# Block-sparse attention and a gated MLP on one core: from split fp32r attention to plain float32 in tiles of the TensorE array

## Chip, cores and metric

One core of one Trainium2 chip runs the whole program. The metric is the time of one execution on the device in microseconds (us), measured as a median over several runs. The profile is one execution recorded by the hardware profiler.

## What is computed

The reference, cut to what matters (4 batches, 8 heads, 768 positions, head size 64; d_model 512, d_ff 1024):

```python
def _attn_ref(q, k, v, n_global, n_local):          # 8 and 96
    scores = scale * np.matmul(q, k.transpose(0, 1, 3, 2))
    is_global = pos[None, :] < int(n_global)
    is_local = (rel >= 0) & (rel < int(n_local))
    keep = is_global | is_local
    scores = np.where(keep, scores + bias, -1e9)    # bias: a slope per head times the distance
    a = softmax(scores)
    return np.matmul(a, v)

def _moe_ref(x, w_in, w_spatial, b_spatial, w_out):
    h = np.maximum(x @ w_in, 0.0)
    u, v = h[..., :d_ff // 2], h[..., d_ff // 2:]
    v_n = (v - mean) / np.sqrt(var + 1e-06)
    v_s = np.einsum('ts,bsd->btd', w_spatial, v_n) + b_spatial[None, :, None]
    return (u * v_s) @ w_out
```

## The kernel before

**Blocks.** Attention goes over 24 blocks of 128 queries, n = 6 b + i (batch b, block i of the batch). A block sees its own 128 keys and the 128 before them, in whose first 32 places the global keys stand, so 256 keys; the first block of a batch sees 128. Heads go in four pairs g: a pair fills the 128 partitions, 64 for each head.

**A block's steps.** prep (L681) loads q and k and prep_v (L718) loads v. scores (L742) multiplies q by k for each head into a PSUM tile of tag "s"; VectorE adds the bias and takes the row's extreme (pr<-s, mn), ScalarE takes the exponential and sums it up (pr<-pr,mn), and GpSimd multiplies by the reciprocal of the sum (pr<-pr,rc), except in batch 0, where that factor is applied to the output ("folded", L664). values (L808) transposes the probabilities on TensorE (p<-ident,pr), copies them to SBUF (pth<-p) and multiplies them by v into ops. The outcome, transposed, is split into an fp32r upper and lower part (xth, xtl), with which the MLP works.

**Two ways through attention.** For batch 0 (whole(n), L660) the products are in plain float32. There q stands in a tile with 64 rows of zeros for the other head, so that a score product uses all 128 rows, and the product with v computes both heads' columns for both heads' probabilities (128 x 256) and uses half. A plain float32 product is two LDWEIGHTS and two MATMUL instructions. For batches 1 to 3, q, k, v and the probabilities are split into two fp32r parts. Six splitting instructions and twelve DMAs per block put q's and k's parts under one another so that the 64 rows of both parts fill 128 rows; a score takes two matmuls, a product with v takes two for each head, and three adds on VectorE and ScalarE (c<-ops) join the parts. TensorE's instructions per full block: 16 for scores and 16 with v, in both ways, and 16 transposes.

**MLP.** mlp_v (V), mlp_u (U), mlp_s (G) and mlp_o (O), L889 to L968, use fp32r in three passes (upper x upper, upper x lower, lower x upper) into PSUM tiles of tag "m". w_in arrives as 64-bit floats and is converted and split by split_weights (L615); so is w_out, and w_spatial is split. This setup (tokens I, Q, T, B) lies in batch 0.

**Order.** Nothing is issued while the kernel is written down: Recorder keeps every operation (L58), plan (L287) simulates the five engines with the costs of cost (L195) and ranks each token by KEYS (L432), and the outcome is one fixed order for every engine. keep_warm (L396) puts transposes of the identity (s<-ident and m<-ident, results that nobody reads) into gaps of TensorE. All instructions are issued at L39, so the profile shows L39 everywhere, and its groups are told apart by tile names. Tensor engine results go to eight PSUM banks: two for each of s, p, ops and m.

## Time and profile before

| | us |
|---|---|
| median of 3 runs | 475.75 |
| lowest and highest run | 473.37, 476.11 |
| span of the profiled execution | 473.8 |
| TensorE busy (matmul) in it | 460.7 |
| VectorE busy | 344.6 |
| ScalarE busy | 279.9 |
| GpSimd busy | 254.1 |

The page lists the span of the profiled execution, from its first to its last instruction, and no other time for it; the span lies within the times of the three runs. PE is the matmul side of TensorE, PEld its weight loads, DVE VectorE, ACT ScalarE, POOL GpSimd, SP the engine that issues DMAs. The end of a matmul in the trace is modelled, so busy shares and means of PE include the tail of one matmul beside the start of the next; the spacing of starts tells what one costs in a run.

### The profile page before, as it was taken

The numbers are of one execution on the slowest core, as the hardware profiler recorded it, in microseconds if no ns is written. First come the engines' busy times: TensorE is split into PE (matmuls) and PEld (weight loads), VectorE is DVE, ScalarE is ACT, GpSimd is POOL, SyncE is SP. The second block draws the span as 40 slices with busy tenths as digits, with TensorE's granted clock in tenths as the row PEclk, the third lists the DMA queues.
The fourth block names the chain that finished last, engine by engine and source line by source line (L and its number), as shares of the span: only waits on it lengthen the run. The fifth ranks groups of instructions, "written<-read, shape, count | busy, mean of one in ns | idle before, by whom it ended". The sixth has DMA issues, their size and how long they took to land.

```text
span 473.8 us, 9730 instructions
## 1 busy us (share of the span) xinstructions
PE 460.7 (97%) x3181; PEld 424.3 (90%) x3181; DVE 344.6 (73%) x1016; ACT 279.9 (59%) x775; POOL 254.1 (54%) x378
## 2 busy tenths in 40 slices
PE   7889999999999999999999999999999999999995
PEld 6668888999999889999999999999989899999994
DVE  6899998948679987986766668784376998843332
ACT  5859896455477776786446448872155888721111
POOL 4334743377575788788545357883037775650000
PEclk9999999999999999999999999999999999999999
DMA  6947323747758687746582167630077683000111
GB/s 212 318 155 229 116 65 114 193 108 183 184 148 226 166 226 193 172 129 166 150 219 101 49 184 187 177 98 19 22 183 209 176 213 78 13 1 1 46 46 50
DMA packets 35915, 65.48 MB, mean 138 GB/s; under 512 B 6064, under 2 KB 6320, under 8 KB 35856
## 3 DMA queue, kind: packets, MB, share of 16 engines
q1 hardware_dynamic: 35856, 64.77, 49.7%
q8 instruction: 27, 0.44, 0.4%
q14 instruction: 32, 0.26, 0.2%
HBM read 29.76 MB, written 6.68 MB: 77 GB/s over the span
## 4 chain that ended last, share of the span: by engine, by line
PE 87%; DVE 4%; SPq 3%; DMA 2%; ACT 2%; issue 1%; DVEq 0%
PE m L39 61%; PE ops L39 9%; PE s L39 9%; PE p L39 8%; SPq L39 3%; DMA vring<-in_v_dram 2%; DVE c L39 1%; ACT pr L39 1%; DVE raw L39 1%; DVE ev L39 0%; DMA kring<-rawh 0%; DVE pr L39 0%; DVE w_in_h L39 0%; DVE rawh L39 0%; DVE xtl L39 0%
## 5 line engine op out<-in xcount | busy, mean ns | idle before, releaser
L39 ACT ACTIVATE pr<-pr,mn 128x256 f32<-128x256 f32 (+1 forms) x192 | 92.0, 483 | 17.5 <-DVE mn L39 17.1
L39 DVE TENSOR_TENSOR c<-ops,c 64x256 f32<-64x256 f32 x168 | 70.6, 421 | 11.0 <-ACT c L39 4.7
L39 DVE CUSTOM_DVE_ANT_0 pr<-s,bias 128x256 f32<-128x256 f32 (+1 forms) x192 | 68.6, 394 | 11.0 <-PE s L39 8.4
L39 POOL TENSOR_SCALAR pr<-pr,rc 128x256 f32<-128x256 f32 (+1 forms) x144 | 68.1, 493 | 10.4 <-DVE rc L39 8.3
L39 PE MATMUL s<-kring,q 128*128 128x256 f32 (+1 forms) x384 | 69.8, 307 | 1.3 <-DVE mn L39 1.0
L39 PE MATMUL ops<-pth,vring 128*128 128x256 f32 x352 | 67.0, 311 | 0.7 <-DVE pth L39 0.5
L39 PEld LDWEIGHTS s<-kring,q 128*128 128x128 f32 x384 | 57.6, 191 | 7.1 <-DVE mn L39 2.4
L39 ACT ACTIVATE pth<-p 128x512 fp32r<-128x512 f32 (+3 forms) x96 | 52.3, 559 | 15.1 <-PE p L39 11.5
L39 PEld LDWEIGHTS ops<-pth,vring 128*128 128x128 f32 x352 | 53.1, 189 | 5.4 <-DVE pth L39 1.2
L39 PE MATMUL p<-ident,pr 128*128 128x128 f32 x352 | 56.6, 273 | 0.7 <-ACT c L39 0.7
L39 DVE TENSOR_TENSOR pth<-p,pth 128x512 fp32r<-128x512 f32 (+1 forms) x72 | 45.1, 642 | 7.0 <-ACT pth L39 6.0
L39 DVE TENSOR_TENSOR ev<-m,b_bc 128x512 f32<-128x512 f32 x24 | 16.6, 691 | 46.1 <-PE m L39 46.0
L39 PEld LDWEIGHTS p<-ident,pr 128*128 128x128 f32 x352 | 42.2, 140 | 5.2 <-ACT c L39 1.3
L39 ACT ACTIVATE ev<-m 128x512 f32<-128x512 f32 (+1 forms) x36 | 21.3, 591 | 42.8 <-PE m L39 40.8
L39 PE MATMUL m<-w_t_h,vnh 128*128 128x256 f32 x288 | 43.9, 282 | 0.0
L39 PE MATMUL m<-w_t_h,vnl 128*128 128x256 f32 x288 | 43.7, 282 | 0.0
L39 PE MATMUL m<-w_t_l,vnh 128*128 128x256 f32 x288 | 43.7, 283 | 0.0
L39 POOL TENSOR_TENSOR xtl<-c,xth 128x256 fp32r<-128x256 f32 x40 | 29.8, 747 | 25.2 <-ACT xth L39 25.1
L39 ACT ACTIVATE gh<-ev 128x512 fp32r<-128x512 f32 x24 | 15.1, 630 | 42.6 <-DVE ev L39 42.6
L39 PEld LDWEIGHTS m<-w_t_h,vnh 128*128 128x128 f32 x288 | 38.9, 189 | 0.7
L39 ACT ACTIVATE c<-ops 64x256 f32<-64x256 f32 x72 | 27.3, 380 | 20.4 <-PE ops L39 17.9
L39 POOL TENSOR_TENSOR vnl<-ev,vnh 128x512 fp32r<-128x512 f32 x24 | 31.1, 1296 | 14.7 <-ACT vnh L39 9.4
(138 smaller groups left out, 997.8 us busy)
## 6 DMA issues: line engine op xcount, KB each, us to landing
q<-rawh SPq DMA_DIRECT2D x72, 128.0 KB, 2.4
q<-raw SPq DMA_DIRECT2D x72, 128.0 KB, 2.4
out_dram<-ev SPq DMA_DIRECT2D x23, 256.0 KB, 2.8
raw<-in_q_dram SPq DMA_DIRECT2D x18, 256.0 KB, 2.9
raw<-in_v_dram SPq DMA_DIRECT2D x18, 256.0 KB, 3.0
raw<-in_k_dram SPq DMA_DIRECT2D x18, 256.0 KB, 3.3
kring<-rawh SPq DMA_DIRECT2D x36, 128.0 KB, 2.4
kring<-raw SPq DMA_DIRECT2D x36, 128.0 KB, 2.4
```

Of the source, the lines that this page charges most:

```text
L39: getattr(self.real, self.call)(*self.args, **self.kw)
```

## The change

All 24 blocks go one way, in plain float32, with no split of q, k, v or the probabilities. q and k are loaded as they lie in memory, one DMA each; v too. The scores of a pair are two float32 products, each of 64 rows (its head's) of the array: tiles in rows. The products with v are of 64 columns each (its head's): tiles in columns. The score products of a whole block (8; in blocks 0 and 1 of half a block) are recorded as one operation `together`, and so are the 16 products with v, after all four transposed tiles are copied. The PSUM banks are now four for s, two for p (in which ops stands too) and two for m. Folding of the reciprocal stays with batch 0 (FOLD). The copy of pth, the normalisation and the upper part of x may go to either of several engines ("x" in CFG). The planner knows of `together`, of a time to change the array's shape, and of new KEYS; so the order of everything is new.

```diff
-CFG = {... 'pth': 'a', ... 'norm': 'p', ... 'xbh': 'a', ... 'b_pth': 2, 'b_c1': 3, ...}
+CFG = {... 'pth': 'x', ... 'norm': 'x', ... 'xbh': 'x', ... 'b_pth': 5, 'b_c1': 2}
...
-BUFS = {"gh": 1, "gl": 1, "u": 3, "s": 2, "p": 2, "m": 2, "raw0": 1, "raw1": 1, "rawh0": 1, "rawh1": 1}
+BUFS = {"gh": 1, "gl": 1, "u": 3, "s": 4, "p": 2, "m": 2, "wos": 2, "wc": 4}
...
+FOLD, SMALL = range(6), 2
+KEYS = {...}
...
     def issue(self):
-        getattr(self.real, self.call)(*self.args, **self.kw)
+        for call, args, kw in self.calls():
+            getattr(self.real, call)(*args, **kw)
...
+        if op.call == "together":
+            return sum(max(2 * elements(kw["rhs"]) * .422, 54) for _, _, kw in op.args), 0, False
...
+def shape_of(op):
+    if op.eng != "tensor":
+        return 0, 0
+    if op.call != "together":
+        return 0, 149 if op.call == "transpose" else 197
+    w = op.args[0][2]["lhsT"]
+    return (1, 197) if list(w.ap)[0][1] < P else (2, 143)
...
+        if e == "tensor" and op.mode != mode:
+            op.busy += op.load
+            mode = op.mode
...
     def prep(n):
...
+        nc.sync.dma_start(out=ring["q", n % 2], in_=q[b, i])
+        nc.sync.dma_start(out=ring["k"][:, n % 3], in_=k[b, i])
+        return ring["q", n % 2]
...
     def prep_v(n):
...
+        nc.sync.dma_start(out=ring["v"][:, n % 3], in_=v[b, i * P:(i + 1) * P, :])
...
     def scores(n, qt):
...
+        PAIRS = 2 if n < SMALL else 4
         for g in range(NP):
             if g == 2:
                 yield
-            sp = ps_s.tile([P, 2, W], F32, name="sp", tag="s")
-            for j in range(2):
-                h = 2 * g + j
-                if whole(n):
-                    nc.tensor.matmul(sp[:, j], lhsT=q1[:, j, g], rhs=kring[:, sl, g], start=True, stop=True)
-                    continue
-                for y, a in enumerate((q1, ql)):
-                    nc.tensor.matmul(sp[:, j], lhsT=a[:, j, g], rhs=kring[:, sl, j, g], start=(y == 0), stop=(y == 1))
+            if g % PAIRS == 0:
+                sp = [ps_s.tile([P, 2, W], F32, name="sp", tag="s") for _ in range(PAIRS)]
+                nc.together(nc.tensor, [
+                    ("matmul", (sp[x // 2 * 2 + j][:, x % 2],), dict(lhsT=qt[s_, g + x], rhs=kring[s_, sl, g + x], start=True, stop=True))
+                    for x in range(PAIRS) for j, s_ in enumerate(halves)
+                ])
...
     def values(n):
...
+            t = work.tile([P, nch, 2, P], F32, name="pth", bufs=nb("pth"))
+            cp(E("pth", g), t, pt)
+            pth.append(t)
...
+        ops = ps_p.tile([P, NP, P], F32, name="ops", tag="p")
+        nc.together(nc.tensor, [
+            ("matmul", (ops[s_, g],), dict(
+                lhsT=vring[:, order[c], g * P + 64 * j:g * P + 64 * j + 64], rhs=pth[g][:, c, j],
+                start=(c == 0), stop=(c == nch - 1),
+            ))
+            for g in range(NP) for c in range(nch) for j, s_ in enumerate(halves)
+        ])
+        if folded(n):
+            xs = work.tile([P, NP, P], F32, name="xs", tag="c1", bufs=nb("c1"))
+            nc.vector.tensor_tensor(out=xs, in0=ops, in1=div, op=ALU.mult)
+            hi_lo(xs, xh[:, :, toks], xl[:, :, toks], E("xf0h"), E("xf0l"))
+        else:
+            hi_lo(ops, xh[:, :, toks], xl[:, :, toks], E("xbh"), nc.vector)
-            pth = work.tile([P, 2 * nch, 2, P], F32R, name="pth", bufs=nb("pth"))
-            hi_lo(pt.rearrange("p c j x -> p (c j) x"), pth[:, :, 0], pth[:, :, 1], E("pth", g), nc.vector)
...
-                for j, s_ in enumerate(halves):
-                    cp(E("c1", j), c1[s_], opsring[j][halves[1 - j], :, 0:P])
-                for j, s_ in enumerate(halves):
-                    nc.vector.tensor_tensor(out=c1[s_], in0=opsring[j][s_, :, P:], in1=c1[s_], op=ALU.add)
-                for j, s_ in enumerate(halves):
-                    nc.vector.tensor_tensor(out=c1[s_], in0=opsring[j][s_, :, 0:P], in1=c1[s_], op=ALU.add)
-                hi_lo(c1, xh[:, gs, toks], xl[:, gs, toks], E("xbh", g // 2), E("xbl", g // 2))
```

## Rows read from the trace of the kernel before

**Rows 1.** The page, part 1: busy us (share of the span) xinstructions.

```profile
PE 460.7 (97%) x3181; PEld 424.3 (90%) x3181; DVE 344.6 (73%) x1016; ACT 279.9 (59%) x775; POOL 254.1 (54%) x378
```

**Rows 2.** Stretches of 25 us from the start: busy time by engine; the answer names the columns.

```profile
core 0: us, PE busy (x) PEld busy (x) DVE busy (x) ACT busy (x) POOL busy (x), PEclk, DMA share, GB/s
0.00:25.00 25.00, 20.54 (x108) 17.11 (x108) 19.15 (x91) 17.38 (x61) 9.03 (x21) 1.00 0.84 266
25.00:50.00 25.00, 22.56 (x125) 18.41 (x123) 24.39 (x68) 18.96 (x56) 12.29 (x12) 1.00 0.55 182
50.00:75.00 25.00, 25.00 (x151) 21.88 (x150) 23.34 (x76) 20.68 (x56) 13.93 (x17) 1.00 0.29 93
75.00:100.00 25.00, 25.00 (x163) 22.93 (x163) 20.23 (x50) 11.61 (x25) 11.78 (x17) 1.00 0.54 144
```

**Rows 3.** TensorE's waits from 50 us on: waiter <- waited for: us, times, longest.

```profile
PE ops L39 <- DVE pth L39: 0.5, 1, 0.5
PE s L39 <- DMA kring<-rawh: 0.2, 1, 0.2
```

**Rows 4.** The chain that ended last, pieces: start us, us, what.

```profile
8.12 9.48 DMA vring<-in_v_dram
...
82.63 1.73 PE ops L39 x8
...
125.98 0.87 PE p L39 x8
...
131.25 0.95 PE s L39 x8
```

**Rows 5.** Timeline, single matmul and weight loads: start us, us, what, [idle before].

```profile
44.80 0.38 PE L39 MATMUL s<-kring,q 128*128 128x256 f32 x1
...
61.43 0.30 PEld L39 LDWEIGHTS ops<-pth,vring 128*128 128x128 f32 x2 [0.28 <-ACT pth L39]
...
17.14 0.20 PEld L39 LDWEIGHTS p<-ident,pr 128*128 128x128 f32 x2 [0.47 <-ACT c L39]
```

**Rows 6.** TensorE's groups by form: xcount | busy us, mean ns of one | idle before.

```profile
L39 PE MATMUL ops<-pth,vring 128*128 128x256 f32 x352 | 67.0, 311 | 0.7 <-DVE pth L39 0.5 <-ACT pth L39 0.2
...
L39 PEld LDWEIGHTS s<-kring,q 128*128 128x128 f32 x384 | 57.6, 191 | 7.1 <-DVE mn L39 2.4 <-POOL xtl L39 0.6 <-issue 0.3
...
L39 PEld LDWEIGHTS p<-ident,pr 128*128 128x128 f32 x352 | 42.2, 140 | 5.2 <-ACT c L39 1.3 <-ACT pth L39 0.4
```

**Rows 7.** Stretches: first the instructions of ops alone, then all, after batch 0's attention.

```profile
0.00:50.00 50.00, 11.01 (x42) 7.34 (x42) 5.03 (x12) 0.00 (x0) 1.00 0.70 224
50.00:84.00 34.00, 11.22 (x46) 8.25 (x46) 4.18 (x10) 0.00 (x0) 1.00 0.31 97
...
84.00:474.00 390.00, 383.65 (x2750) 358.76 (x2748) 270.16 (x766) 217.61 (x593) 216.63 (x326) 1.00 0.49 131
```

**Rows 8.** VectorE's and ScalarE's groups by form, columns as in rows 6.

```profile
L39 DVE TENSOR_TENSOR c<-ops,c 64x256 f32<-64x256 f32 x168 | 70.6, 421 | 11.0 <-ACT c L39 4.7 <-ACT pth L39 1.3 <-PE ops L39 1.0
L39 DVE CUSTOM_DVE_ANT_0 pr<-s,bias 128x256 f32<-128x256 f32 x160 | 60.8, 416 | 6.1 <-PE s L39 4.8 <-POOL xtl L39 0.5 <-PE p L39 0.3
L39 DVE TENSOR_TENSOR pth<-p,pth 128x512 fp32r<-128x512 f32 x60 | 40.2, 687 | 5.0 <-ACT pth L39 4.2
...
L39 DVE TENSOR_TENSOR ev<-m,b_bc 128x512 f32<-128x512 f32 x24 | 16.6, 691 | 46.1 <-PE m L39 46.0
...
L39 DVE DVE_READ_ACCUMULATOR2_ANT mn<- 128x1 f32 x192 | 15.7, 82 | 0.0
...
L39 DVE TENSOR_TENSOR raw<-raw,rawh 128x512 fp32r<-128x512 f32 x15 | 13.1, 876 | 0.1
...
L39 ACT ACTIVATE pth<-p 128x512 fp32r<-128x512 f32 x60 | 34.5, 594 | 8.6 <-PE p L39 6.6 <-PE ops L39 1.1
```

**Rows 9.** The page, part 6: DMA issues by tile, xcount, KB each, us to landing.

```profile
q<-rawh SPq DMA_DIRECT2D x72, 128.0 KB, 2.4
...
kring<-rawh SPq DMA_DIRECT2D x36, 128.0 KB, 2.4
```

## Prediction

> **What bounds the kernel now.** I read the page first: PE is busy 460.7 of 473.8 us, and no other engine over 73% [rows 1]. Busy PE is not yet PE at its limit, so I went to the stretches and then to TensorE's waits. [...] Ahead of 50 us it is otherwise: there TensorE is busy 43.1 of 50 us, and VectorE 24.39 of 25 from 25 to 50 us [rows 2].

> [...] The chain gives the spacing of matmuls, as a run of n divided by n [rows 4]: a plain float32 pass (batch 0; every float32 product is two of them) over 256 columns 1.73/8 = 0.216 us; a split fp32r matmul over 256 columns 0.95/8 = 0.119; a transpose 0.87/8 = 0.109. One matmul's record is 0.38 us long at a spacing of 0.216 [rows 5]: the remaining 0.16 us is a tail that overlaps with the next. Two loads of 128 columns of weights with nothing before them lie 0.30 - 0.19 = 0.11 us apart; for the transposes, 0.20 - 0.14 = 0.06 [rows 5, 6]. In a run these loads hide: the spacing stays at 0.216.

> **What the change removes from TensorE.** Attention's products are 384 instructions of scores and 352 with v [rows 6]. Batch 0 (float32, 96 and 88 of them): scores 80 x 0.216 = 17.3 and 16 narrow ones (128 columns) at half, 1.7; v 88 x 0.216 = 19.0; together 38.0 us. Batches 1 to 3: scores 240 x 0.119 = 28.6 and 48 narrow ones, which cannot go below their 0.11 us load, 5.3; v 264 x 0.119 = 31.4; together 65.3. In all 103.3 us. The transposes stay.

> **What it adds.** A block of 128 queries has 8 float32 score products (two passes each) over 256 columns, each in 64 rows of the array. No row of before shows two tiles at work. If the tiles overlap fully, a product costs one spacing of 0.216 rather than two, so 1.73 us a block; in the four first blocks of a batch, with 128 keys, half. With v there are 16 products of 128 columns in 64 array columns, so 32 passes of 0.108, two at a time: 1.73 us too. That is 20 x 1.73 + 4 x 0.86 = 38.0 for each kind, 76.1 in all: 19.0 for batch 0, 57.1 for the others. The other end is no overlap, 152.2. I take full overlap: the plain float32 rows show a pass at 0.216 with a hidden load of 0.11, and in the tiles the loads (two of 0.11 a score product, two of half that a v product) still fit into the streaming, barely.

> The second addition is the change of the array's shape. There are 26 groups of scores (two in each of blocks 0 and 1, then one a block) and 24 with v, so 50 groups and 100 changes if none are neighbours. A change must at least expose a first load (0.055 or 0.11, mean 0.08), and at most the 0.16 us tail and the load (0.245) [rows 5, 6]. I take the middle, 0.16, since no row shows one: 16 us, 4.5 of them in batch 0 (28 changes) and 11.5 later (72).

> Batch 0 thus goes from 38.0 to 23.5 (-14.5), batches 1 to 3 from 65.3 to 68.6 (+3.3). The split fp32r path was already as cheap on TensorE as the tiles: 16 x 0.119 = 1.9 us against 1.73. The gain is all in batch 0.

> [...]

> **What batch 0 can keep.** Of its 88 products with v, 42 lie ahead of 50 us [rows 7], where TensorE was not full; there its gain, 14.5 x 42/88 = 7.0 us, stays only as far as the engine that holds it up gets faster. That is VectorE. It loses 24 sums of c at 0.421 (10.1 us) [rows 8] and gains 6 of 512 columns out of PSUM, at 0.69 as the add of b_bc [rows 8], 4.1: 6.0 us less over the batch, half of it, 3.0, ahead of 50 us. So 4.0 us become idle time. The bounds are 0 (GpSimd, busy 12 to 14 of 25 us there [rows 2], takes over some splits in the new plan) and 14.5 - 6.0 = 8.5 (VectorE sets the pace until batch 0 is done).

> **What costs nothing.** In batches 1 to 3 VectorE loses the lower halves of pth (40.2 us and the narrow ones), 144 sums of c (60.5) and the splits of q and k (13.1) [rows 8], and gains 18 subtractions out of PSUM of 0.69 (12.4); ScalarE and GpSimd lose the splits of v and the copies of c, SP the scattering DMAs of q and k (72 and 36, and as many of the lower parts) [rows 9]. All this lies beside a full TensorE (383.65 of 390 us) [rows 7]: nothing won. Two waits are new. A group of scores needs all four s banks, so the eight evacuations of the block before (8 x 0.5 = 4 us) [rows 8]; a group with v needs all four copies of pth (4 x 0.59 = 2.4 us of ScalarE) [rows 8]. Behind either on TensorE's queue stand MLP passes, which all of MLP's results wait for. A block lasts 390/18 = 21.7 us after batch 0 [rows 7], all but some 5.5 of them (2 x 1.9 and 16 x 0.109) MLP passes that can be put between; uncovered, the two would cost up to 6 us a block. I take nothing, and leave it in the range. For DMA, one load of q replaces two in batch 0; the first v load was waited for until 17.6 us [rows 4], and still is.

> Sum: span 473.8 - 14.5 + 3.3 + 4.0 = 466.6 us. The median of the runs is 475.75, 1.95 above that span (the lowest run 0.4 below); with 1.95 added the forecast is **468.5 us**, 1.5% faster.

> **Rivals.**
> [...]
> 2. *VectorE holds batch 0 up.* For it: 24.39 and 23.34 of 25 us [rows 2]. Against: from 50 us TensorE was full with MLP passes, and more of these can come forward. Batch 0 keeps 6.0 us: 473.8 - 6.0 + 3.3 + 1.95 = 473.0.
> 3. *The tiles do not overlap* (the other side; the tiling does not do what it says). Each pass then holds the whole array: +76.1, 544.6 us. It decides early: with all groups 9% longer than 1.73 us (83.3 us in all) the gain is gone (103.3 - 16 - 4.0). Against it: the two tiles use separate rows, or columns, and write to separate banks or partitions.
> 4. *The loads of the v tiles are exposed.* If a load could not run beside a matmul that uses the same rows, each of 704 passes with v would add 0.0535 us: +37.7, 506.2 us. Against it: in the trace a load of 0.11 us hides under a spacing of 0.216 in the same 128 rows [rows 4, 5]. [...]

> **How the numbers follow.** Forecast 0.58, rival 1 0.15, rival 2 0.12, rival 3 0.08, rival 4 0.05; 0.02 is left. The likeliest case alone: from 456.5 (changes at 0.08, nothing given back) to 475. About 1% is what a measurement of this kernel can tell from no change. Faster by over 1% (under 471.0): most of the forecast, 0.55. Within 1%: rival 2, two thirds of rival 1, a little of the forecast: 0.27. Slower: rivals 3 and 4 and the rest of rival 1, 0.18. The range reaches down to 456 for cheap changes and up to 482 for rival 1 with dear ones; rivals 3 and 4 lie outside.

> **What would show it.** The forecast is right if a group of 16 score passes spans about 1.73 us and a group of 32 with v the same, if a change of shape leaves a gap of 0.1 to 0.2 us beyond the usual spacing, if TensorE still waits under 2 us after 60 us, and if VectorE falls by some 110 us at no use. Batch 0's attention should end near 74 to 78 us (now 84.4 [rows 4]). It is wrong if such groups span 1.9 us or more, if TensorE waits for pth or for s banks in each block, or if its idle time ahead of 84 us grows by 8 us.

## The result and the profile after

The changed kernel takes 464.54 us (463.98 to 464.74), the kernel before 475.73: a ratio of 0.9766, 95% interval 0.9732 to 0.9799, so 2.3% faster. The forecast was 468.5, between 456 and 482. The profiled execution spans 462.2 us, 11.6 less than before.

The page of the changed kernel, part 1; its counterpart is [rows 1]:

```profile
PE 449.2 (97%) x3570; PEld 401.0 (87%) x3570; DVE 281.8 (61%) x926; ACT 215.4 (47%) x615; POOL 101.6 (22%) x156
```

TensorE has 389 more instructions and is busy for 11.5 us less; GpSimd loses 60% of its work, and that is not what the time follows. Stretches of the changed kernel, columns as in [rows 2], the last one behind 84 us as in [rows 7]:

```profile
0.00:25.00 25.00, 19.53 (x159) 16.13 (x161) 18.48 (x86) 17.00 (x57) 6.66 (x17) 1.00 0.78 287
25.00:50.00 25.00, 22.97 (x201) 18.20 (x197) 24.82 (x80) 21.60 (x64) 13.25 (x12) 1.00 0.62 198
50.00:75.00 25.00, 24.41 (x228) 21.07 (x225) 22.63 (x80) 20.52 (x65) 15.36 (x18) 1.00 0.42 133
75.00:100.00 25.00, 25.00 (x205) 21.69 (x204) 23.22 (x87) 18.69 (x59) 10.83 (x18) 1.00 0.28 88
...
84.00:462.00 378.00, 373.32 (x2918) 337.77 (x2916) 207.97 (x653) 149.15 (x408) 61.35 (x102) 1.00 0.16 53
```

TensorE is full from 75 us until its last matmul, 5.1 us ahead of the end (before: from 50). Behind 84 us VectorE is busy for 55% of the stretch, GpSimd for 16%; the TensorE time that is missing there lies behind that last matmul. Its waits from 50 us on are one line, as in [rows 3]:

```profile
PE p L40 <- ACT pth L40: 0.5, 1, 0.5
```

What a group costs stands in the chain (start us, us, what); the first piece is a block's scores, the second its products with v:

```profile
62.77 1.93 PE s L40 x16
64.70 1.90 PE p L40 x32
```

A piece runs from its first start to the first start of what follows, so it includes one change of the array's shape. Sixteen passes of 256 columns in 1.93 us are 0.12 each, where a pass alone takes 0.216 [rows 4]: two tiles stream at once. A timeline of the changed kernel, cut to 0.1 us, shows it directly (start us, us, engine, what):

```profile
181.34 0.70 PE L40 MATMUL s<-kring,q 64*128 64x256 f32 x4
```

Four matmuls have started by 181.80 and end within 0.70 us of the first. The records behind this line start at 181.337 and 181.343, then 181.657 and 181.663, and from there two every 0.216 us, 6 to 7 ns apart. In a v group the pairs come every 0.109.

One more change is in the groups of fillers, the transposes of the identity (columns as in [rows 6]):

```profile
L40 PE MATMUL s<-ident 128*128 128x128 f32 x45 | 7.6, 337 | 1.7 <-POOL ident masks.py:199 1.7
...
L40 PE MATMUL m<-ident 128*128 128x128 f32 x22 | 2.6, 273 | 0.0
...
L40 PE MATMUL p<-ident 128*128 128x128 f32 x11 | 1.6, 277 | 0.0
```

There are 78 of them where 41 stood before, since the planner puts them into gaps of the start-up and the new plan has more of these.

**Where the time went.** Adding up, over each trace, the distance from every matmul's start to the next one's, by kind:

| us | before | after | difference |
|---|---|---|---|
| scores, v and transposes | 145.2 | 129.2 | -16.0 |
| fillers | 7.0 | 14.5 | +7.5 |
| MLP | 313.0 | 311.6 | -1.4 |
| ahead of the first, from the last on | 8.6 | 6.8 | -1.8 |
| span | 473.8 | 462.2 | -11.6 |

Waits count here for the kind that stands ahead of them, so a wait in the start-up can hide in any row. Scores and v alone fall by 24.7 us (110.4 to 85.7), and the transposes rise by 8.7, since gaps and changes of shape now stand behind them. Attention as a whole gives 16.0 us; the fillers take 7.5 back, and 3.2 are saved elsewhere. Split by batch, attention falls from 55.4 to 40.1 us in batch 0 and from 89.7 to 89.1 in batches 1 to 3: the gain lies in batch 0.

### The profile page after: what moved, and what is told of

It is laid out like the page before. It is cut to its first block, busy times and chain, and to the rows that moved or that the text cites. A ratio compares the mean times of both kernels' runs of the same rounds, so it can differ in the third digit from the quotient of the medians.

```text
span 462.2 us, 9460 instructions
## 1 busy us (share of the span) xinstructions
PE 449.2 (97%) x3570; PEld 401.0 (87%) x3570; DVE 281.8 (61%) x926; ACT 215.4 (47%) x615; POOL 101.6 (22%) x156
## 4 chain that ended last, share of the span: by engine, by line
PE 89%; DVE 6%; ACT 3%; DMA 1%; issue 1%; SPq 0%; ACTq 0%; DVEq 0%
PE m L40 65%; PE p L40 16%; PE s L40 8%; DVE wc L40 1%; DVE pr L40 1%; ACT pr L40 1%; DMA nraw<-in_n_local_dram 1%; DVE c L40 1%; ACT pth L40 1%; DVE bias L40 0%; ACT wc L40 0%; DVE ev L40 0%; DVE pth L40 0%; DVE xtl L40 0%; DVE w_in_l L40 0%
## 5 line engine op out<-in xcount | busy, mean ns | idle before, releaser
L40 ACT ACTIVATE pr<-pr,mn 128x256 f32<-128x256 f32 (+1 forms) x192 | 92.0, 483 | 13.8 <-DVE mn L40 12.4
L40 ACT ACTIVATE pth<-p 128x512 f32<-128x512 f32 (+1 forms) x80 | 43.6, 558 | 22.8 <-PE p L40 16.8
L40 PEld LDWEIGHTS p<-ident,pr 128*128 128x128 f32 x352 | 40.1, 140 | 13.0 <-ACT pth L40 3.5
L40 PE MATMUL s<-kring,q 64*128 64x256 f32 (+1 forms) x384 | 45.1, 372 | 2.2 <-DMA kring<-in_k_dram 1.7
L40 POOL TENSOR_TENSOR rs<-mv,eps 128x1 f32<-128x1 f32 x24 | 5.2, 218 | 178.5 <-DVE mv L40 177.4
L40 PE MATMUL p<-pth,vring 128*64 128x128 f32 x704 | 43.7, 276 | 0.3 <-ACT pth L40 0.3
L40 PEld LDWEIGHTS p<-pth,vring 128*64 128x64 f32 x704 | 37.9, 137 | 6.4 <-issue 4.0
L40 PEld LDWEIGHTS s<-kring,q 64*128 64x128 f32 x384 | 33.7, 186 | 9.7 <-issue 3.4
L40 DVE TENSOR_SCALAR pr<-pr,rc 128x256 f32<-128x256 f32 (+1 forms) x115 | 39.3, 397 | 0.4
L40 PEld LDWEIGHTS m<-w_t_h,vnl 128*128 128x128 f32 x288 | 38.1, 189 | 0.0
L40 PEld LDWEIGHTS m<-w_t_l,vnh 128*128 128x128 f32 x288 | 37.8, 188 | 0.0
L40 DVE BATCH_NORM_STATS2 st<-ev 128x6 f32<-128x512 f32 x24 | 16.5, 690 | 33.9 <-ACT ev L40 33.7
```

The costliest lines, as they stand in the source:

```text
L40: getattr(self.real, call)(*args, **kw)
```

## The experiments

**1. Overlap undone.** The order of the calls inside a group is changed, nothing else:

```diff
+        calls = self.calls()
+        if self.call == "together":
+            calls = [*calls[0::2], *calls[1::2]]
+        for call, args, kw in calls:
```

> Inside each group of tiled matmuls, all products of the first tile are issued ahead of all products of the second, so that two neighbours never use different tiles; the plan and everything else stay. Theory A (the gain is TensorE time, and it rests on two tiles streaming at once): each full group goes from about 1.73 to 3.46 us of streaming, 20 x 2 x 1.73 + 4 x 2 x 0.86 = 76 us more, so about 535 to 541 us. Rival B (the matmuls' close starts in the trace are only records, the gain is the other engines' relief or the new order): within 3 us of 464.5.

Measured: 510.15 us in one run, 45.6 more. The direction is theory A's, the size is not; rival B is out. Two pieces of this kernel's chain, the groups of one block (the second piece has two transposes behind the 32 passes):

```profile
201.76 2.89 PE s L43 x16
204.65 3.62 PE p L43 x34
```

2.89 against 1.93 is 0.96 more, not 1.73. The records say why. Eight passes of the first tile are issued ahead of the second tile's eight, but the second tile's first one starts 6 ns after the fifth, while three passes issued ahead of it have not started; in the v group it starts 6 ns after the 13th of 16. So four passes of each tile still overlap. Of the scores 12 passes stand one after another where eight did: 4 x 0.216 us, and 0.10 since the second tile's first step is as long as the first tile's (0.32). That is 0.97, as measured from first to last start (2.59 against 1.62). With v it is 12 x 0.109 and 0.05, so 1.36 (3.055 against 1.695). Over the 20 full blocks these make 46.6 us. In the whole trace, short blocks included, scores and v take 48.6 us more, and its span is 46.2 us longer.

**2. More changes of shape.** In each of 22 score groups a transpose is put in the middle, which adds 44 changes to the 79 of the changed kernel:

```diff
+                for x, (call, args, kw) in enumerate(op.args):
+                    if x == 4:
+                        bare.tensor.transpose(args[0][:, 0:P], ident, ident)
+                    getattr(op.real, call)(*args, **kw)
```

> The changed kernel, its order kept; in each of the 22 groups of 8 score products one transpose of the identity is put in the middle (into an s bank that the group's second half overwrites), so the array's shape changes there and back. Theory A (a change costs about 0.15 us and TensorE is full): 0.11 for the transpose and 2 x 0.15, so 0.40 us a group; 18 groups lie behind the start-up, 7.3 us, and 4 more in it, up to 1.6: 471.5 to 473.5 us. Rival I (the change itself is nearly free and only the loads show): 0.16 to 0.2 a group, 468 us or less.

Measured: 475.24 us, 10.7 more. Rival I is out; theory A is right in kind, and a little low. The chain shows one such group:

```profile
188.41 1.06 PE s L991 x8
189.47 0.26 PE s L990
189.73 1.06 PE s L991 x8
```

2.38 us against 1.93, so 0.45, of which 0.11 are the transpose: 0.17 us a change. With the whole run it is (10.7/22 - 0.11)/2 = 0.19, but that includes the start-up, where the granted clock fell to 0.93 between 25 and 50 us.

The records of the changed kernel show the same without any edit. Behind a group of scores the first pair with v starts 0.306 us after the last pair of scores, where 0.216 is usual, and the next pair 0.160 after it, where 0.109 is usual: 0.14 together. Ahead of a group of scores the two are 0.09 and 0.10 longer, so 0.20.

**3. Tiles in batch 0 alone.** The kernel before and its ranks, with tiles (two pairs to a group) in batch 0:

```diff
+            if whole(n):
+                if g % 2 == 0:
+                    sps = [ps_s.tile([P, 2, W], F32, name="sp", tag="s") for _ in range(2)]
+                    nc.together(nc.tensor, [...])
```

> The kernel before, with its own ranks, where only batch 0 uses tiles: q in one load, scores of two pairs as one group in row tiles, products with v of two pairs as one group in column tiles; batches 1 to 3 keep the split fp32r way. Theory A (batch 0 carries the gain, the later batches are even): 24 groups in batch 0 rather than 12 or 14 cost some 3 us more in changes of the array's shape than the change has there, so about 466 to 470 us. Rival C (the later batches carry the gain): 473 us or more, near the kernel before.

Measured: 513.91 us, a ratio of 1.0787 (1.0753 to 1.082). Neither theory foresaw that, and the run does not decide between them. Its three largest TensorE waits behind 100 us, where the code is that of before:

```profile
PE m L40 <- ACT xth L40: 9.8, 4, 4.2
PE m L40 <- ACT ev L40: 5.4, 5, 3.5
PE ops L40 <- DVE c L40: 3.6, 1, 3.6
```

The kernel before has 0.7 us of waits from 50 us on [rows 3]; here they add up to some 22 us, and the granted clock falls to 0.93 between 150 and 250 us. The ranks were made for another list of operations, and the plan that comes of them leaves TensorE idle in the later batches. That the ranks are the reason is likely, and not shown by this run. So the order became the next question.

**4. The order.** Ranks exchanged or left out, no other edit:

```diff
-KEYS = {'start': -231.15, ('P', 0): -197.34, ...}
+KEYS = {'start': -18.36, ('P', 0): -14.95, ...}      # of the kernel before; in the next two runs: {}
```

> The changed kernel with the ranks (KEYS) of the kernel before, so that the plan is made anew from old ranks. Theory A (TensorE's sum carries the gain; order matters in the start-up alone): 464 to 471 us. Rival D (the new order is the gain): 475 us or more.

> The changed kernel without ranks: the planner falls back on the order in which the program is written down. Theory A (TensorE's sum carries the gain, the order is found equally well for both kernels): it rises as much as the kernel before does without its ranks, and the ratio between the two stays near 0.976. Rival H (with less work on the other engines the order matters less): it rises by 12 us or less, to under 477.

> The kernel before without ranks, beside the changed kernel without ranks. Theory A: it rises as the changed one does, their ratio near 0.976. Rival H: it rises by 20 us or more, to over 496, since its VectorE, ScalarE and GpSimd have less room to make up for a poor order.

Measured: 484.36 us for the changed kernel with the ranks of before (1.0189 of the kernel before, 1.0162 to 1.0216); 474.85 without ranks (0.9979, 0.9965 to 0.9993); and 502.14 for the kernel before without ranks (1.0544, 1.0496 to 1.0592). For the first, theory A fails, and the time is one that rival D allows: with ill-fitting ranks the change is 1.9% slower than the kernel before. Yet the next two runs speak against D itself, since the change does not need its own ranks to be ahead. For them rival H holds: without ranks the changed kernel rises by 10.3 us, the kernel before by 26.4, and their ratio is 474.85/502.14 = 0.946, not 0.976. The stretch from 200 to 300 us, first of the kernel before, then of the changed one, both without ranks:

```profile
200.00:300.00 100.00, 92.65 (x622) 83.40 (x622) 72.69 (x212) 61.42 (x175) 65.62 (x97) 0.97 0.60 158
```

```profile
200.00:300.00 100.00, 100.00 (x774) 88.69 (x773) 58.27 (x200) 48.22 (x137) 14.28 (x26) 1.00 0.19 61
```

Without its ranks the kernel before leaves TensorE idle for 7.35 us of these 100, and the granted clock falls to 0.97; the changed one stays full. So the changed kernel bears a poor order better. I put that down to the relief of its other engines. That is argued, not shown: its PSUM banks are shared out in another way too, and no run takes the two apart. With well-chosen ranks both kernels are full there, and it buys nothing.

**5. Normalisation back on GpSimd.**

```diff
-'norm': 'x'
+'norm': 'p'
```

> The changed kernel with the normalisation of batches 1 to 3 on GpSimd alone, as before (115 of 144 are on VectorE now, 39 us). Theory A (behind the start-up the other engines hide under a full TensorE): 462.5 to 466.5 us, not to be told from the change. Rival B (the relief of other engines pays): 468 us or more.

Measured: 465.8 us (465.6 to 466.6), 1.3 above the change and within the range of theory A; rival B is out. 115 of its 144 multiplications moved back.

**6. What paces the start-up.** Four runs with the order kept: without fillers, then also without the 24 VectorE instructions on w_in, in the changed kernel and in the one before.

```diff
-            if gap > WARM_GAP and op.begun < WARM_TO:
+            if False:
...
-            op.issue()
+            if getattr(op, "num", None) not in dropped:     # the instructions on w_in
+                op.issue()
```

> The changed kernel, its order kept, without the 78 transposes of the identity that fill TensorE's gaps in the start-up. Theory E (the fillers stand in idle time only, and VectorE sets the pace there): within 2 us of 464.5, with a granted clock of 1.00 or a little lower in the first 50 us. Rival F (the 14.5 us that the fillers take are themselves the loss): 455 us or less.

> As the run without fillers, and the 24 VectorE instructions that rebuild w_in's low bits are left out (some 16 us of VectorE in the first 66; the output is another). All other instructions keep their order. Theory E (VectorE paces batch 0, TensorE has room): 6 us or more under the run without fillers. Rival G (the DMA of the weights and of v, or ScalarE, paces batch 0): within 2 us of it.

> The kernel before, its order kept, without its 41 fillers: the mark for the next run. Theory E: within 2 us of 475.7.

> The same omission as in the changed kernel (24 VectorE instructions on w_in, no fillers), made in the kernel before; order kept. Theory E (before the change TensorE itself was nearly full until 84 us, so VectorE's share of the pace was smaller): 2 to 5 us under the kernel before without fillers, so less than the changed kernel gains. Rival G: within 2 us of it, and the same in both kernels.

Measured, changed kernel: 466.16 without fillers, 468.24 with the lighter VectorE too. Kernel before: 478.12 and 474.62. The fillers cost nothing: rival F is out. They stand in idle time, and the run without them takes 1.6 us more. The changed kernel without them from 10 to 30 us, then with them from 20 to 30:

```profile
10.00:20.00 10.00, 6.66 (x34) 5.19 (x33) 6.53 (x38) 7.53 (x32) 3.23 (x5) 0.94 1.04 396
20.00:30.00 10.00, 9.90 (x81) 7.74 (x81) 8.87 (x25) 5.72 (x15) 0.62 (x1) 0.72 0.49 179
```

```profile
20.00:30.00 10.00, 9.25 (x74) 6.44 (x75) 9.90 (x31) 6.35 (x16) 1.94 (x3) 1.00 0.68 230
```

Without fillers the granted clock from 20 to 30 us is 0.72 rather than 1.00, after ten microseconds in which TensorE was busy for 6.66 us alone; with them it was busy for 8.43 of the same ten. For the changed kernel theory E falls: VectorE is busy for 12.0 us less in the first 70 (46.69 rather than 58.71), and the run takes 2.1 us more. The kernel before gets 3.5 us faster, as theory E said, but its clock rose too, from 0.84 to 1.00 between 10 and 20 us, which may be worth up to 1.6 of them (0.16 x 10, an estimate). The lower clock blurs these runs, so I took out more, with the fillers in place:

> The changed kernel with its order and its fillers kept; the whole rebuilding of w_in from 64-bit floats is left out, 32 VectorE or GpSimd and 8 ScalarE instructions (about 19 us of VectorE and 5.4 us of ScalarE ahead of 66 us; the split that follows reads constants, and the output is another). Theory J (VectorE and ScalarE pace batch 0 together): 3 to 6 us less, about 459 to 462. Rival K (the fixed order and the chain from engine to engine within a block pace it, no engine's load does): within 2 us of 464.5.

```diff
+        start = len(nc.ops)
         nc.scalar.activation(c, upper.bitcast(F32), AF.Abs)
...
+        if w == FH:
+            dropped.update(range(start, len(nc.ops)))
```

Measured: 463.49 us, 1.1 less, which lies within rival K's range and short of theory J's. From 25 to 50 us:

```profile
25.00:50.00 25.00, 22.20 (x178) 18.56 (x176) 17.69 (x63) 19.76 (x59) 12.00 (x12) 0.93 0.55 181
```

VectorE went from 24.82 to 17.69 of 25 us and TensorE gained nothing (22.20 us busy rather than 22.97). Batch 0's attention ends at 66.8 us, in the change at 66.6. But the clock is lower here too, at 0.93, which may hide up to 1.75 us (0.07 x 25, an estimate); a run whose mean clock was 0.999 took 462.3. So under this order the loads of VectorE and ScalarE hold the start-up up by less than 3 us. GpSimd's load and the transfers were not lightened, and whether a plan made for lighter engines would use the room was not tried.

## Why the prediction was right

**The bound.** The forecast counts TensorE from 50 us on, and only its time. Before, TensorE was busy in the whole of each 25 us from 50 to 100 at a granted clock of 1.00 [rows 2], with 0.7 us of waits from 50 us on [rows 3]; after, these waits are 0.5 us. So it was right for these two orders. It does not hold in general that nothing else counts: in experiment 4, where the order is poor, 27 us lie between the two kernels.

**Full overlap.** It was taken on thin evidence, and it was right: a pair of score passes comes every 0.216 us, a pair with v every 0.109, and experiment 1 shows what its loss costs. Rivals 3 and 4 are out, and so is rival 1, for which the forecast has a chance of 0.15 and a range up to 482 us: weight loads that lengthen the passes in tiles. No run shows such a term; the pairs came at these 0.216 and 0.109 us. That the loads still fit in, "barely", was too careful: no load shows behind a group's first step. By rival 4's count (0.0535 us more for each pass) a v pair would have come every 0.216 us. Both v tiles use the same 128 rows, and the pair came every 0.109 us. "Groups of 1.9 us or more" was named as a sign that the forecast is wrong; the pieces are 1.93 and 1.90, but a change of shape is in them.

**The price of a change.** I took 0.16 us from bounds, an estimate that no row of before shows; experiment 2 gives 0.17, and the records 0.14 to 0.20, by what follows. A whole tail and load (0.245), the upper bound, is not paid.

**The number of changes.** This is the mis-sized term. I counted 100, "if none are neighbours"; the trace has 79, since 17 times a block's scores stand right beside products with v and one change serves both, and in blocks 0 and 1 the two half groups share theirs. 79 x 0.16 = 12.6 us, not 16: 3.4 of the 4.0 us by which the forecast was too high. TensorE's part is then 103.3 - 76.1 - 12.6 = 14.6 of gain rather than 11.2; the table has 16.0, and the rest, 1.4, is not worked out. One term in the 103.3 was too strict: the narrow scores of batches 1 to 3 were put at no less than their 0.11 us load, a floor that no run shows; in the trace of before they start 0.057 to 0.061 us apart in 9 of 38 steps, some 0.5 us in all. Batches 1 to 3 were to lose 3.3; with the 53 changes behind the start-up, 65.3 would become 65.6, so they come out even, and so the trace has it (89.7 and 89.1 us, transposes included).

**What batch 0 gives back.** The forecast was 4.0 us. By the table it is 16.0 - 11.6 = 4.4. By another count, ahead of 84 us TensorE's idle time went from 6.9 to 8.1 us and 37 more fillers of 0.109 us are some 4, so about 5 in all. The size was about right, and that was partly luck, for two steps to it were wrong. I took the share ahead of 50 us from products with v alone (42 of 88); of the scores 72 of 96 lay there, which would have made it some 6 us. And I put it on VectorE, but a lighter VectorE did not bring it back (experiment 6). The plan also did something that I had not thought of: it pulled all of batch 0's attention ahead of the MLP, so that it ends at 66.6 us and not at 74 to 78, with 28 MLP matmuls done by then (98 before, by 84.0). Why the start-up has more gaps than before is open beyond that.

**Other engines.** VectorE fell by 63 us, not by some 110: the planner moved 115 normalisations (39.3 us) and some copies of pth onto it. It was at no use, as forecast: with the normalisations back on GpSimd the time is within 1.3 us (experiment 5).

## What to carry to other kernels

Where TensorE is full, count its time alone, and count plain float32 in two 64-row or 64-column tiles at half its price (here a pair of score passes came every 0.216 us, as a single untiled pass did, and a pair with v, of half the columns, every 0.109) plus the 0.14 to 0.20 us that a change of shape took here. Put tiled groups of different kinds side by side, so that one change serves both, as it did 17 times here. Compare two kernels only with orders made for each: foreign ranks cost the changed kernel 20 us, more than the change brings. What a change is worth depends on the order: 11.2 us lie between these kernels with their own ranks, 27.3 without any.
